# Key-value products of a gated linear recurrence: row tiles of 64 tokens with 112 columns in place of four quarter tiles

## The chip, the cores and the metric

The kernel runs on one core of a Trainium2 chip. The metric is the device time of one execution in microseconds, the median of several runs. A core has a matrix engine (TensorE, in the profile PE, with its weight loads as PEld), a vector engine (VectorE, DVE), a scalar engine (ScalarE, ACT), a general engine (GpSimd, POOL) and a queue engine (SyncE, SP) which here issues most DMAs. Each engine works through its own instructions in order and waits on the others by semaphores.

## The reference

Two blocks follow each other: a gated recurrence with complex gates, for 4 batches, 8 heads, 768 tokens and 48 numbers a head, and a mixer with a low-rank product over the tokens and a two-layer product over the channels. Cut to its core:

```python
for t in range(S):                     # gates a normalised to a magnitude of at most 0.999
    new_re = ar * S_re - ai * S_im
    new_im = ar * S_im + ai * S_re
    kv = np.einsum('bhd,bhe->bhde', k[:, :, t], v[:, :, t])
    S_re, S_im = (new_re + kv, new_im)
    y[:, :, t] = np.einsum('bhd,bhde->bhe', q[:, :, t], S_re)
x = y.transpose(0, 2, 1, 3).reshape(B, S, H * D)
...
h = x.transpose(0, 2, 1) @ U @ V                      # U: 768 x 32, V: 32 x 768
u = x + h.transpose(0, 2, 1)
out = u + np.maximum(u @ w_ch1, 0.0) @ w_ch2          # 384 -> 1536 -> 384
```

## The kernel before

The recurrence is done in chunks of 128 tokens: 6 chunks for each of 4 batches, 24 in all, each for all 8 heads. Gates become running phases and magnitudes; queries and keys are multiplied by them, so that what is left in a chunk are plain products. For a chunk the steps are:

- `prep`: VectorE weighs q and k and makes QKC, which has for every token and head two parts u = 0, 1 (48 numbers each, one for the cosine, one for the sine), each in a place of 64 columns, so that the two parts stand in columns 0 to 47 and 64 to 111; columns 48 to 63 hold zeros. TensorE turns it (`tr`, line 816) in row tiles of 64 tokens: two tiles, one for each half of the chunk, side by side in the array.
- `inner` (line 845): products of keys and queries within each half, masked by VectorE into AT.
- `state` (line 865): the key-value products, the step that is changed. For each head h and half r, the weights are k's 64 tokens by a part's columns and the moving operand is the values' 64 tokens by 48 numbers (VP). The sum over the 64 tokens goes to dk[r], rows 0 to 63 for part 0 and rows 64 to 111 for part 1. It is issued in two operations of 4 heads each. In the last chunk of a batch only half 0 is needed. The array is used as four tiles of 64x64, (half, part).
- VectorE adds dk[0] and dk[1] to the running state G, with the state at the middle of the chunk in GM (for the first chunk of a batch, ScalarE copies GM instead).
- `y` (lines 894 and 902): products of AT with the values and of the queries with the states, copied by ScalarE into xo.

The mixer takes two chunks at a time (groups m = 0 to 11): `rank` and `mixed` (lines 937 and 960) for the low-rank part, `rT` and `rw` for a correction of the first group, `uTp` for the turned input, then the two-layer product. Group 0 does it plainly; from group 2 on, `few` (line 1103) does the first layer with fewer products, and from group 1 on `down_two` (line 1235) does the second layer with fewer products out of sums of the weights; VectorE makes these sums, one of them at line 1305 for the first such group (m = 1), in place over a part of w2.

The order of the work is written out by hand, or rather by a planner before: every step is added to a list with its engine, an estimated cost, and `way`, the form in which it splits TensorE's array (0 the whole array, 1 column tiles, 3 four quarter tiles, 4 row tiles of 32, 5 row tiles of 64). `ORDER` is the order in which the 2210 listed operations are emitted, on all engines; the estimates stand in the code but play no part in the emitted program. `SPARE` names operations before which dummy products on an identity matrix are emitted (`idle`, lines 1383 and 1387); 34 of them in all.

A tile takes part in the semaphores by the framework's own account of reads and writes; the lists of reads and writes in the plan only check the order.

Of the kernel before, what the change touches and what calls it, by code (L numbers as in the profile page):

```python
# [19 lines left out]
HC = CH // 2  # L20
# [94 lines left out]
)  # L115

SPARE = {
    125: 2, 135: 10, 199: 14, 209: 1, 223: 5, 243: 2,
}

DUMP = None
# [195 lines left out]
def kernel(  # L317
# [15 lines left out]
    nc = tc.nc  # L333
    B, H, S, D = q.shape
    DP = 64
# [1119 lines left out]
```

## Time and profile before

| | us |
|---|---|
| median of 3 runs | 555.26 (554.55 to 555.47) |
| the profiled execution | 554.71 |
| its span, first to last instruction | 552.8 |
| TensorE busy in the span | 526.9 (95%) |
| VectorE busy | 432.8 (78%) |
| ScalarE busy | 317.8 (57%) |
| GpSimd busy | 32.2 (6%) |
| mean granted TensorE clock | 0.998 |

How the profile's views are read: in the page's 40 slices a digit is the busy share of a slice in tenths. Groups of instructions have the line, engine, operation, output and inputs by name, the shape (for a product the weights' rows*columns, then the moving operand's rows and columns), the count, and then the busy time in us, the mean duration of one in ns, and the idle time before them with what ended it. The chain of work that ended last, in order of time, has a start in us, a length in us, and what it was. A row of waits names who waited for whom, the us in total, the number of times and the longest. A timeline has a start, a length, and the instructions merged in it. Products are pipelined: one of 0.22 us may start 0.015 us after another.

### The profile page before, as it was taken

What the parts mean: (1) busy time and instruction counts of PE and PEld (TensorE: products, weight loads), DVE (VectorE), ACT (ScalarE), POOL (GpSimd) and SP (SyncE); (2) the same over time, 40 slices, a digit from 0 to 9 for tenths busy, and PEclk for the clock granted to TensorE, in tenths of its full rate; (3) what the DMA queues carried; (4) which work ended last, traced back from release to release, by engine and by line L of the source; (5) the groups of instructions that cost most, each with busy time, mean ns of one, the idle gap of its engine ahead of it and who ended that gap; (6) DMA issues with size and microseconds to landing.
All of it is one profiled execution on the core that took longest, in us unless ns stands there. A gap on an engine that the chain in (4) does not pass through costs nothing.

```text
span 552.8 us, 16672 instructions
## 1 busy us (share of the span) xinstructions
PE 526.9 (95%) x7228; PEld 477.3 (86%) x7228; DVE 432.8 (78%) x828; ACT 317.8 (57%) x553; POOL 32.2 (6%) x61
## 2 busy tenths in 40 slices
PE   2899999999999999999999999999999999999996
PEld 1677776767999987999999998999999989999995
DVE  6899989999999987998787987786953635567352
ACT  6889999795597787567827956626512232110100
POOL 1000000001010000102001001002000000000000
PEclk9999999999999999999999999999999999999999
DMA  9988876523441354314513425003300000000001
GB/s 229 187 184 174 195 170 151 144 30 87 88 89 30 56 104 77 59 31 85 91 38 67 74 38 111 2 1 59 59 9 23 17 11 15 8 8 23 21 9 34
DMA packets 150688, 39.92 MB, mean 72 GB/s; under 512 B 145912, under 2 KB 147408, under 8 KB 150608
## 3 DMA queue, kind: packets, MB, share of 16 engines
q1 hardware_dynamic: 148400, 34.43, 31.2%
q0 software_dynamic: 2208, 4.35, 2.3%
q8 instruction: 59, 0.97, 0.7%
q14 instruction: 21, 0.17, 0.1%
HBM read 33.60 MB, written 4.76 MB: 69 GB/s over the span
## 4 chain that ended last, share of the span: by engine, by line
PE 73%; DVE 12%; ACT 4%; issue 2%; DMA 1%; POOL 0%; DVEq 0%; SPq 0%; ACTq 0%; POOLq 0%
PE down L1235 26%; PE few L1103 25%; PE tr L816 4%; PE dk L865 3%; PE inner L845 3%; PE y L902 3%; PE up L991 2%; PE y L894 2%; DVE xo L444 1%; ACT gate L438 1%; PE rank L937 1%; PE ph L755 1%; PE mixed L960 1%; PE uTp L976 1%; PE es ps L691 1%
## 5 line engine op out<-in xcount | busy, mean ns | idle before, releaser
L1111 ACT COPY h<-few 128x512 f32<-128x512 f32 x60 | 35.1, 585 | 87.3 <-PE few L1103 87.1
L1235 PE MATMUL down<-w,h 128*128 128x192 f32 x396 | 72.7, 330 | 0.9 <-DVE xo L444 0.7
L438 ACT ACTIVATE gate<-gate 128x768 f32<-128x768 f32 (+2 forms) x74 | 65.6, 900 | 9.2 <-DVE GS L750 3.8
L1235 PEld LDWEIGHTS down<-w,h 128*128 128x128 f32 x396 | 64.5, 190 | 3.7 <-issue 1.5
L822 ACT COPY QK<-tr 112x512 f32<-112x512 f32 x96 | 49.9, 596 | 17.8 <-PE tr L816 17.7
L444 DVE TENSOR_TENSOR xo<-down,xo 128x192 f32<-128x192 f32 (+1 forms) x79 | 29.9, 385 | 33.9 <-PE down L1235 33.4
L1115 DVE CUSTOM_DVE_ANT_1 h<-few,h 128x512 f32<-128x512 f32 x60 | 40.5, 686 | 15.7 <-PE few L1103 11.8
L1103 PE MATMUL few<-extra,w 128*128 128x128 f32 x400 | 50.9, 276 | 0.0
L1103 PEld LDWEIGHTS few<-extra,w 128*128 128x128 f32 x400 | 48.0, 192 | 0.1
L441 DVE TENSOR_TENSOR QKC<-qk,cs 128x768 f32<-128x768 f32 x48 | 44.4, 950 | 1.7 <-PE dk L865 1.3
L1235 PE MATMUL down<-stage 128*128 128x192 f32 x198 | 37.9, 330 | 0.4 <-DVE xo L444 0.4
L438 ACT ACTIVATE es<-es ps 128x384 f32<-128x384 f32 x48 | 20.1, 502 | 31.2 <-PE es ps L691 29.2
L444 DVE TENSOR_TENSOR h<-few,h 128x512 f32<-128x512 f32 x30 | 20.6, 688 | 20.4 <-ACT h L1111 12.1
L1179 POOL DMA_DIRECT2D out_dram<-xo x32 | 17.9, 558 | 313.8 <-DVE xo L444 297.7
L991 PE MATMUL up<-uT,w 128*128 128x256 f32 x144 | 34.5, 387 | 0.7 <-ACT uT L980 0.7
L1235 PEld LDWEIGHTS down<-stage 128*128 128x128 f32 x198 | 32.3, 190 | 1.7 <-DVE xo L444 1.0
L1103 PE MATMUL few<-gate,w 128*128 128x128 f32 x240 | 32.2, 278 | 0.4 <-DVE gate L1075 0.4
L435 ACT ACT_TABLE_LOAD x24 | 30.8, 1283 | 1.1 <-PEq L1439 0.7
L816 PEld LDWEIGHTS tr<-ident,QKC 64*112 64x112 f32 x768 | 24.2, 130 | 8.3 <-issue 3.6
L816 PE MATMUL tr<-ident,QKC 64*112 64x64 f32 x768 | 28.9, 221 | 2.4 <-DVE QKC L441 2.4
L991 PEld LDWEIGHTS up<-uT,w 128*128 128x128 f32 x144 | 26.4, 190 | 5.3 <-ACT uT L980 0.9
L1103 PEld LDWEIGHTS few<-gate,w 128*128 128x128 f32 x240 | 29.3, 192 | 0.8 <-PE uTp L976 0.6
(161 smaller groups left out, 1100.4 us busy)
## 6 DMA issues: line engine op xcount, KB each, us to landing
stage<-in_moe_w_ch_dram SPq DMA_DIRECT2D x12, 768.0 KB
gate<-in_a_im_dram SPq DMA_DIRECT2D x24, 192.0 KB
gate<-in_a_re_dram SPq DMA_DIRECT2D x24, 192.0 KB
VP<-in_v_dram SPq DMA_DIRECT2D x24, 192.0 KB
qk<-in_q_dram SPq DMA_DIRECT2D x24, 192.0 KB
qk<-in_k_dram SPq DMA_DIRECT2D x24, 192.0 KB
out_dram<-xo POOLq DMA_DIRECT2D x12, 192.0 KB, 2.2
out_dram<-xo POOLq DMA_DIRECT2D x20, 96.0 KB, 2.1
```

What stands on the lines that cost most here:

```text
L435: ACT(1.4, rank, lambda: nc.scalar.preload_act_table_set(name), writes=[TABLE])
L438: return nc.scalar.activation(out=o, in_=i, func=f, **kw)
L441: nc.vector.tensor_tensor(out=o, in0=a, in1=b, op=OP.mult)
L444: nc.vector.tensor_tensor(out=o, in0=a, in1=b, op=OP.add)
L816: nc.tensor.transpose(out=get(*ps[r])[0:DQ, h], in_=get(*qkc)[at, h].rearrange("p u d -> p (u d)")[:, 0:DQ], identity=ident[at, at], tile_ ...
L822: nc.scalar.copy(out=get(*QK)[:, u].rearrange("p (h t) -> p h t", t=CH)[:, :, r * HC:(r + 1) * HC], in_=get(*ps[r])[0:DQ])
L991: nc.tensor.matmul(out=get(*ps)[:, e], lhsT=w1[:, f, (ff + e) * 128:(ff + e + 1) * 128], rhs=get(*uT)[:, f], start=(f == 0), stop=(f == KD ...
L1103: nc.tensor.matmul(out=get(*ps)[:, q], lhsT=w()[:, q * 128:(q + 1) * 128], rhs=v[0](), start=(n == 0 and q == 0), stop=True, skip_group_ch ...
L1111: ACT(c_act(n3 * CH) - 0.045, RU, lambda i=i, k=k: nc.scalar.copy(out=at(i, k), in_=get(*ps)), [ps], [o])
L1115: DVE(c_dve(n3 * CH), RU, lambda i=i, k=k: nc.vector._custom_dve(dve_ops.TENSOR_ADD_SAT, out=at(i, k), in0=get(*ps), in1=at(i, k), s0=math ...
L1179: queue.dma_start(out=out[b, c * CH:(c + 1) * CH, lo:hi], in_=get("xo", i)[:, lo:hi])
L1235: nc.tensor.matmul(out=get(*to)[:, part], lhsT=x(j), rhs=y[:, j], start=(first and j == 0), stop=(j == KH - 1), skip_group_check=not first)
```

## The change

The state products are no longer four tiles for each head but two: the two parts of a head, with the 16 columns of zeros between them, are taken as one operand of 112 weight columns, and the two halves of the chunk stand as row tiles of 64 tokens side by side, as in the transposes of line 816. The outputs are the same rows of dk[r]; rows 48 to 63 now hold zeros from the product itself.

```diff
             for h in range(h0, h0 + HH):
                 for r in parts_k:
                     at = slice(r * HC, (r + 1) * HC)
-                    for x, end in ((0, DP), (DP, DQ)):
-                        nc.tensor.matmul(out=get(*dk[r])[x:end, h], lhsT=get(*ks)[at, h, x // DP, 0:end - x], rhs=get(*VPi)[at, h],
-                                         start=True, stop=True, tile_position=(r * HC, x))
+                    nc.tensor.matmul(out=get(*dk[r])[0:DQ, h], lhsT=get(*ks)[at, h].rearrange("p u d -> p (u d)")[:, 0:DQ],
+                                     rhs=get(*VPi)[at, h], start=True, stop=True, tile_position=(r * HC, 0))
         for h0 in (0, HH):
-            PE(0.443, RR, lambda h0=h0: state(h0), [ks, VPi], [dk[r] + (h0,) for r in parts_k], way=3,
-               steps=4 * HH * len(parts_k),
+            PE(0.4, RR, lambda h0=h0: state(h0), [ks, VPi], [dk[r] + (h0,) for r in parts_k], way=5,
+               steps=2 * HH * len(parts_k),
                takes=[mid_G] + ([] if last else [G]))
```

The order of all work is replaced by another one made for these estimates, of the same 2210 operations. On TensorE 505 of 624 operations stand at another place of its list, by 7 places in the mean and 56 at most; on VectorE 667 of 793, on ScalarE 422 of 553, on GpSimd 15 of 48, on SyncE 143 of 192. The dummy products are 32 instead of 34:

```diff
 SPARE = {
-    125: 2, 135: 10, 199: 14, 209: 1, 223: 5, 243: 2,
+    125: 3, 135: 10, 199: 15, 209: 1, 227: 2, 253: 1,
 }
```

One product of `down_two` names a further read, so that it comes after the vector operation of line 1305, which makes the weights it uses:

```diff
             onto(ub, 1, two, 0)
-            product(one, 0, lambda j: of(0, 1)[:, j], w2_of(0, 1), names, first=False)
+            product(one, 0, lambda j: of(0, 1)[:, j], w2_of(0, 1), lambda half: names(half) + [("w2", 0)], first=False)
             onto(ub, None, one, 0)
```

169 rows, old and new, of the table ORDER are left out of this document.

## The prediction

> **What bounds the kernel now.** I read first the page's busy shares and its 40 slices, then the chain that ended last, then what TensorE waited for.
>
> ```profile
> span 552.8 us, 16672 instructions
> PE 526.9 (95%) x7228; PEld 477.3 (86%) x7228; DVE 432.8 (78%) x828; ACT 317.8 (57%) x553; POOL 32.2 (6%) x61
> PE   2899999999999999999999999999999999999996
> DVE  6899989999999987998787987786953635567352
> ACT  6889999795597787567827956626512232110100
> PEclk9999999999999999999999999999999999999999
> PE 73%; DVE 12%; ACT 4%; issue 2%; DMA 1%; POOL 0%; DVEq 0%; SPq 0%; ACTq 0%; POOLq 0%
> ...
> PE es ps L695 <- DVE GL L444: 11.0, 1, 11.0
> PE tr L816 <- DVE QKC L441: 2.4, 3, 1.6
> PE ph L758 <- ACT gate L438: 1.4, 3, 0.8
> PE down L1235 <- DVE xo L444: 1.3, 4, 0.7
> PE ph L761 <- DVE F L764: 1.2, 2, 0.6
> PE dk L865 <- issue: 0.8, 2, 0.5
> PE up L991 <- ACT uT L980: 0.7, 1, 0.7
> PE ph L755 <- PE tr L816: 0.4, 1, 0.4
> ...
> PE down L1235 <- issue: 0.2, 1, 0.2
> ```
>
> TensorE is busy in 95% of the span, nine tenths in each slice but the first and last few, at a granted clock that never falls, and 73% of the chain is its own. Of what it waited for, 11.0 us is the wait for the first gates before its first product. All others of that list come to about 10 us (2.4 + 1.4 + 1.3 + 1.2 + 0.8 + 0.7 and, from the row of 0.4 to that of 0.2, six small ones of 2.0 in all). So from 11 us on TensorE is a queue that is hardly ever empty. A change of its own work goes nearly whole into the time, and the question is only what the key-value products cost in each form.
>
> **What they cost now.** Each of the 8 heads of a chunk has two halves of 64 tokens (r) and two parts (x, with 64 and 48 columns of weights). The rows by shape say in how many instructions each product is issued:
>
> ```profile
> L865 PE MATMUL dk<-VP,QKC 64*64 64x48 f32 x704 | 27.7, 221 | 0.3 <-issue 0.3
> L865 PE MATMUL dk<-VP,QKC 64*48 64x48 f32 x704 | 24.9, 214 | 0.5 <-issue 0.5
> ...
> 160.97 1.07 PE dk L865 x56
> 236.90 2.00 PE dk L865 x120
> 446.15 1.99 PE dk L865 x89
> ```
>
> 20 chunks do both halves and the last chunk of each of 4 batches one: 8 x (20 x 2 + 4) = 352 products of each part, and 704 instructions, so two passes for each. A chunk is thus 64 instructions (the chain keeps some 56 of them), and takes 1.07 us when it stands alone; two chunks in a row take 2.00. So the work itself is 0.93 us, 0.058 for each group of four instructions that run side by side on the four 64x64 tiles, and 0.14 us is the entry and exit of a run. The last row is a whole chunk and a last one: 1.99 - 1.07 = 0.92 for a last chunk, although it has half the instructions. A group with two tiles idle thus takes as long as one with four; what counts is groups. Sum now: 20 x 0.93 + 4 x 0.92 = 22.3 us.
>
> **What they cost after.** One product now has 112 weight columns, 64 rows, and the same 48 moving columns. Two of them (r = 0 and 1) stand side by side. A chunk is 8 heads x 2 passes = 16 groups, as before; the number of instructions halves (1408 to 704), that of groups stays at 24 x 16 = 384. So everything hangs on the time of a group. No row has a plain product of this form; these are nearest:
>
> ```profile
> L816 PEld LDWEIGHTS tr<-ident,QKC 64*112 64x112 f32 x768 | 24.2, 130 | 8.3 <-issue 3.6 <-DVE QKC L441 2.5 <-DVE xo L444 0.2
> L976 PEld LDWEIGHTS uTp<-ident,xo 128*128 128x128 f32 x72 | 8.5, 141 | 2.8 <-DVE xo L444 0.8 <-ACT QK L822 0.6 <-ACT es L438 0.4
> L865 PEld LDWEIGHTS dk<-VP,QKC 64*48 64x48 f32 x704 | 21.8, 119 | 0.0
> L865 PEld LDWEIGHTS dk<-VP,QKC 64*64 64x64 f32 x704 | 24.6, 135 | 3.0 <-issue 1.4 <-DVE AT L848 0.2
> L960 PEld LDWEIGHTS mixed<-r,V 64*128 64x128 f32 x96 | 8.1, 186 | 1.9 <-ACT r L943 0.8 <-issue 0.6 <-PE ph L755 0.3
> L1005 PEld LDWEIGHTS rT<-both,r 64*128 64x128 f32 x6 | 0.8, 188 | 0.0
> L1005 PE MATMUL rT<-both,r 64*128 64x32 f32 x6 | 0.7, 258 | 0.0
> ...
> 92.28 0.41 PEld L1005 LDWEIGHTS rT<-both,r 64*128 64x128 f32 x3
> 96.46 0.30 PEld L960 LDWEIGHTS mixed<-r,V 64*128 64x128 f32 x4 [0.17 <-issue]
> ...
> 49.18 1.04 PE tr L816 x32
> 309.64 1.48 PE tr L816 x48
> 251.99 0.89 PE few L1103 x8
> ```
>
> Weight loads of plain products grow with their columns: 119 ns for 48, 135 for 64, 186 to 188 for 128, about 0.8 ns a column, and the number of rows makes no difference (rT and mixed have 64 rows). How often a tile can take one is the next row: three loads of rT, 128 columns each, last 0.41 us; less the 0.188 of the last one that is two steps of 0.111, though their products move only 32 columns (64x32 in the row of rT's products). The "few" products have 128 weight columns and 128 moving ones and take 0.89 / 8 = 0.111 as well. So with few moving columns the load sets the step: 0.111 at 128 columns, 0.058 at 64. In a straight line between these, 112 columns give 0.058 + 48/64 x 0.053 = 0.098 us. The two halves do load side by side: four loads of mixed, two for each half, are over in 0.30 us, which is one step of 0.111 and a last load of 0.186; one after another they would need 0.52.
>
> The transposes of line 816 have the very shape, 64x112, and cost (1.48 - 1.04) / 8 = 0.055 for a pair. But they are no measure: their load of 112 columns takes 130 ns, less than the 135 of a plain one of 64, and the transposes of line 976 load 128 columns in 141 where plain products need 186 and more. A transpose loads at about half price. I take 0.098 and keep 0.055 (the transposes) and 0.111 (all of 128 columns) as ends.
>
> Sum after: 384 x 0.098 = 37.6 us, 15.3 more than now. With the ends: 384 x 0.055 = 21.1 (1.2 less) and 384 x 0.111 = 42.6 (20.3 more).
>
> **The other parts of the change.** The order of all work is new. I counted neighbours in the list of TensorE's 624 operations whose form of tiling (the number "way" in the code) differs: 160 before and 147 after, where a state operation counts as row tiles like the transposes. A run of dk has 0.14 us for its two ends, 0.07 for each: 13 x 0.07 = 0.9 us gained. Against it, a run of plain row tiles is dearer to enter:
>
> ```profile
> 213.31 0.88 PE mixed L960 x8
> 475.95 1.50 PE mixed L960 x16
> ```
>
> 8 instructions more are 0.62 us here, so 0.26 lie at the ends, 0.12 more than for dk. 29 of the 48 ends of dk runs still meet another form, 29 x 0.06 = 1.7 us; since mixed has 128 columns and a longer stream I take 1.0 (0 to 1.7). The dummy products between operations (SPARE) go from 34 to 32, each of two instructions of 0.111: 0.4 us gained.
>
> The added dependence on ("w2", 0) makes one product of the second mixer group wait in the plan for the vector subtraction at line 1305; that one keeps its place in the list (594th before, 593rd after), the product too (701st, 704th), 100 operations later. It costs nothing. Should that distance go, the product would stand behind one vector operation of 1.27 us:
>
> ```profile
> 132.48 1.27 DVE w L1305
> ```
>
> What waits for the state products is the vector engine's sum GM; it ends at most 0.64 us later for each chunk (16 x 0.098 - 0.93), and that sum's readers are later TensorE work in the same queue, which is late by as much. So nothing else becomes late by it. The other engines do gain: VectorE at 78% and ScalarE at 57% have 15 us more for the same work, so some waits of TensorE shrink. All those waits after the first product are 10 us; many follow TensorE's own products (xo from down) and stay. I take 2 us for this and for what the new order does to waits, between 0 and 10; a new order can lose as well, and its planner put a state operation at 0.4 us where I expect 0.78 (8 x 0.098), so I give it no gain beyond.
>
> The sum, against the profiled execution's own 554.7 us (552.8 of span and 1.9 around it; the median of the runs is 555.3, 0.5 higher and inside their spread): 554.7 + 15.3 - 0.9 + 1.0 - 0.4 - 2.0 = 567.7. I predict 567.5 us, 2.2% slower.
>
> **The rivals.** *The load is as cheap as the transposes'.* Then a group takes 0.055, and the time is 554.7 - 1.2 - 0.9 - 0.4 = 552.2 (551 to 554.5): faster. It decides at one place, the step of two row tiles with 112 weight columns: below (22.3 + 1.3) / 384 = 0.061 us the kernel is faster, above it slower. For it speaks the same shape in line 816; against it the loads of rT and mixed, plain products in the same row tiling, at 186 to 188 ns. [...]
>
> *The loads don't overlap.* If the second half's load or the second pass's waits for the first's, a group takes up to 0.196; for whole chunks 20 x 16 x 0.196, for last ones 4 x 16 x 0.098, together 69.0 us, and the time is 554.7 + 46.7 - 1 = about 600. Against it: the four loads in 0.30 us. A form of it with part of the load in sight would end between 575 and 600.
>
> *The work is hidden.* If the waits shrink by all of their 10 us, or the new order saves as much, the time is 567.7 - 8 = about 559.5 (557 to 560.5, since other terms can be a little less). Against it: the slices of TensorE are full to the end, while VectorE's and ScalarE's are at 7 tenths and less in the last ten, so that there is little left there for it to wait for.
>
> **Chances.** Forecast, a step set by a load of 112 columns and mostly in sight: 0.82, with 560 to 573. As cheap as the transposes or as before: 0.10. Loads in a row, wholly or in part: 0.04. Hidden: 0.04. The range 559.5 to 573 holds the first and some of the last: its low end has 8 us of waits gone, its high end the dear step of 0.111 (20.3 instead of 15.3). A difference below 0.2%, 1.1 us, can't be told from no change here. Faster by more is the cheap load, 0.08; within it 0.02, where that case is eaten by the order; slower 0.90.
>
> **What would show it.** Profile after: dk in one group, 704 weight loads of 64x112 of about 175 ns (135 + 48 x 0.83), against 130 if the cheap load holds. The chain's runs of one chunk at about 1.6 to 1.8 us, two in a row some 1.57 more (cheap: 0.9; in a row: 3.1). TensorE still at 95% or more, with its waits at 10 us less a few. The prediction is wrong if that step is below 0.09 or above 0.115 us, or if the waits change by over 5 us either way.

## The result, and the profile after

| | us |
|---|---|
| before, median of 4 runs beside the changed kernel | 555.37 (554.55 to 557.82) |
| changed, median of 4 runs | 567.76 (566.60 to 571.68) |
| ratio | 1.0229, 95% interval 1.0201 to 1.0256 |
| changed, another time, 4 runs against 13 of before | 568.28 against 555.95, ratio 1.0247 (1.0210 to 1.0283) |
| profiled executions of the changed kernel | 571.68 (span 569.9) and 566.08 (span 564.3) |

The change costs 12.4 us. First the page of the first profiled execution: the span, TensorE's busy time, its 40 slices and its granted clock, and the two rows of the state products, now in one form.

```profile
span 569.9 us, 15239 instructions
PE 544.6 (96%) x6520; PEld 495.6 (87%) x6520; DVE 434.9 (76%) x828; ACT 319.0 (56%) x553; POOL 32.1 (6%) x61
PE   2799998999999999999999999999999999999996
PEclk9978999999999999999999999999999999999999
L865 PE MATMUL dk<-VP,QKC 64*112 64x48 f32 x704 | 43.6, 265 | 0.4 <-ACT gate L439 0.4
L865 PEld LDWEIGHTS dk<-VP,QKC 64*112 64x112 f32 x704 | 41.0, 180 | 2.9 <-ACT gate L439 1.0
```

Half as many products and loads (704 instead of 1408), and 43.6 us of busy time where the two old forms had 27.7 and 24.9, which overlapped. TensorE is as full as it was, so that it still bounds the kernel. New is the granted clock: it falls in the third and fourth slice. In the second profiled execution it falls only once before the end, and that is the cleaner one to read the steps from. Its weight loads, its chain in order of time (start, us, what) and its waits:

```profile
L865 PEld LDWEIGHTS dk<-VP,QKC 64*112 64x112 f32 x704 | 39.6, 174 | 2.9 <-ACT gate L439 1.0 <-issue 1.0
...
247.24 3.28 PE dk L865 x64
282.69 1.56 PE dk L865 x32
287.96 1.70 PE dk L865 x32
...
PE es ps L696 <- DVE GL L445: 10.1, 1, 10.1
PE tr L817 <- DVE QKC L442: 2.8, 2, 2.5
PE ph L759 <- ACT gate L439: 1.2, 1, 1.2
```

A chunk that stood alone with 1.07 us now takes 1.70, or 1.56 where it follows the transposes, whose tiling it shares. Two in a row take 3.28: 1.58 for a chunk, 0.098 to 0.099 for each of its 16 groups. A weight load takes 174 ns, where the 135 ns of 64 columns and 48 more columns at 0.83 ns had given 175; the transposes' load of the same shape had 130 before. The wait for the first gates is 10.1 us, 0.9 less than before.

### The profile page after: what moved, and what is told of

Read it like the earlier page. It is cut to its first block, busy times and chain, and to the rows that moved or that the text cites. A ratio compares the mean times of both kernels' runs of the same rounds, so it can differ in the third digit from the quotient of the medians.

```text
span 569.9 us, 15239 instructions
## 1 busy us (share of the span) xinstructions
PE 544.6 (96%) x6520; PEld 495.6 (87%) x6520; DVE 434.9 (76%) x828; ACT 319.0 (56%) x553; POOL 32.1 (6%) x61
## 4 chain that ended last, share of the span: by engine, by line
PE 70%; issue 11%; ACT 4%; DVE 4%; DMA 2%; POOL 1%; POOLq 0%; DVEq 0%; ACTq 0%
PE down L1235 22%; PE few L1103 19%; PE dk L865 5%; PE up L991 5%; PE inner L846 3%; PE down L1192 3%; PE tr L817 3%; PE y L902 2%; DMA gate<-F 2%; ACT gate L439 2%; PE y L894 2%; PE mixed L960 1%; PE uTp L976 1%; PE ph L759 1%; PE ph L756 1%
## 5 line engine op out<-in xcount | busy, mean ns | idle before, releaser
L823 ACT COPY QK<-tr 112x512 f32<-112x512 f32 x96 | 50.2, 596 | 28.2 <-PE tr L817 27.9
L865 PE MATMUL dk<-VP,QKC 64*112 64x48 f32 x704 | 43.6, 265 | 0.4 <-ACT gate L439 0.4
L865 PEld LDWEIGHTS dk<-VP,QKC 64*112 64x112 f32 x704 | 41.0, 180 | 2.9 <-ACT gate L439 1.0
L817 PEld LDWEIGHTS tr<-ident,QKC 64*112 64x112 f32 x768 | 26.5, 138 | 6.9 <-DVE QKC L442 3.4
```

The source lines that it names most:

```text
L817: nc.tensor.transpose(out=get(*ps[r])[0:DQ, h], in_=get(*qkc)[at, h].rearrange("p u d -> p (u d)")[:, 0:DQ], identity=ident[at, at], tile_ ...
L823: nc.scalar.copy(out=get(*QK)[:, u].rearrange("p (h t) -> p h t", t=CH)[:, :, r * HC:(r + 1) * HC], in_=get(*ps[r])[0:DQ])
L865: nc.tensor.matmul(out=get(*dk[r])[0:DQ, h], lhsT=get(*ks)[at, h].rearrange("p u d -> p (u d)")[:, 0:DQ], rhs=get(*VPi)[at, h], start=True ...
```

## The experiments

Seven runs were made, the changed kernel once more and six other kernels; each has its ratio to the kernel before on the same chip.

**The changed kernel again.** No edit.

> The changed kernel once more, for a second profile and as the base of the runs beside it. Theory L (the load of 112 weight columns sets a step of 0.098 us, and nearly all of 384 x 0.040 = 15.3 us is in sight): 566 to 569 us, TensorE's step for a pair of row tiles 0.098. The first profile showed a granted clock of 0.73 between 25 and 50 us; theory C (the change itself lowers the clock at the start, by more waits there): low again, clock at most 0.99 in every profile; theory L has no need of it: clock above 0.995 in some.

568.28 us, ratio 1.0247. The step is 0.098 (above). The granted clock of the eight executions of the changed kernel so far was 0.987 to 0.997, never above, against 0.995 to 1.000 in all but one of the 13 of before taken with them (that one had 0.946 and 563.33 us). So 566 to 569 held, and the 0.995 was reached in some, against theory C; yet there is a loss of clock that theory L doesn't know. The stretches around the one fall of the second profile (length, then busy time and count by engine, then the granted clock, the share of the DMA engines and GB/s):

```profile
25.00:28.70 3.70, 2.65 (x52) 2.50 (x54) 3.70 (x6) 3.12 (x5) 0.00 (x0) 1.00 1.36 233
28.75:32.10 3.35, 3.35 (x48) 3.00 (x46) 2.77 (x7) 2.93 (x5) 0.00 (x0) 0.50 1.05 277
32.20:40.00 7.80, 6.84 (x158) 5.60 (x154) 7.36 (x15) 5.89 (x11) 0.00 (x0) 1.00 0.89 192
```

The clock is halved for one stretch of 3.4 us, right after the first chunk's state products, and then whole again. They need not be the cause: in the first profile the fall begins at 25.7 us, ahead of the first state product at 27.8.

**The form in the old order.** The changed state products, with ORDER and SPARE as before. The operation's estimate and the further read of `down_two` are those of the changed kernel too; the cut shows the products alone. Against the kernel before:

```diff
                     at = slice(r * HC, (r + 1) * HC)
-                    for x, end in ((0, DP), (DP, DQ)):
-                        nc.tensor.matmul(out=get(*dk[r])[x:end, h], lhsT=get(*ks)[at, h, x // DP, 0:end - x], rhs=get(*VPi)[at, h],
-                                         start=True, stop=True, tile_position=(r * HC, x))
+                    nc.tensor.matmul(out=get(*dk[r])[0:DQ, h], lhsT=get(*ks)[at, h].rearrange("p u d -> p (u d)")[:, 0:DQ],
+                                     rhs=get(*VPi)[at, h], start=True, stop=True, tile_position=(r * HC, 0))
```

> The new form of the key-value products in the order and with the dummy products of before. Theory L: the whole loss is the form's: +15.3 for the load, -1.2 for 17 changes of tiling form fewer (143 against 160, 0.07 us each), +1.0 for dearer entries, -2 of waits: 567 to 569 us. Rival O (part of the loss is the new order's, which was made for a cost of 0.4 us where it is 0.78): at least 3 us below the changed kernel. Rival P (the new order pays part of the form back): at least 3 us above it.

567.52 us, ratio 1.0218 (1.0144 to 1.0292): the changed kernel's time, 0.8 us below its median. Its four executions lie in two pairs, 565.26 and 565.34 at a clock of 1.000 and 569.71 and 571.74 at 0.990 and 0.987, so that the interval is wide, 8 to 16 us. The median has neither O nor P, which asked for 3 us below or above: most of the loss is the form's, but this run alone can't tell a share of 3 us. Its executions also have 2.7 to 3.1 us outside the span, where those of the other kernels have 1.8 or 1.9; why isn't known. By the mean spans the form alone costs 11.3 us (565.1 against 553.8).

**The new order with the old form.** The reverse: the new ORDER and SPARE with the four quarter tiles. Against the changed kernel:

```diff
                     at = slice(r * HC, (r + 1) * HC)
-                    nc.tensor.matmul(out=get(*dk[r])[0:DQ, h], lhsT=get(*ks)[at, h].rearrange("p u d -> p (u d)")[:, 0:DQ],
-                                     rhs=get(*VPi)[at, h], start=True, stop=True, tile_position=(r * HC, 0))
+                    for x, end in ((0, DP), (DP, DQ)):
+                        nc.tensor.matmul(out=get(*dk[r])[x:end, h], lhsT=get(*ks)[at, h, x // DP, 0:end - x], rhs=get(*VPi)[at, h],
+                                         start=True, stop=True, tile_position=(r * HC, x))
```

> The four quarter tiles of before in the new order, with the new dummy products. Theory L: as before, 555 us within 1.5 (165 changes of tiling form against 160 cost 0.35, two dummy products fewer save 0.4). Rival O: 558 and more. Rival P: 552.5 and less.

557.17 us over 10 runs against 555.95, ratio 1.0031 (1.0010 to 1.0053). The order alone costs 1.2 us by the medians and 0.6 to 2.9 by the interval: small, but not nothing, and the median is inside the 1.5 that L allowed and less than O gave. The two parts, 2.2% and 0.3%, are together what the change shows, within the intervals; by the mean spans they are 11.3 and 1.6 us, and the changed kernel's is 12.7. The stretch from 25 to 50 us in this kernel's profile (length, busy time and count by engine, clock, DMA):

```profile
25.00:50.00 25.00, 21.62 (x411) 17.05 (x412) 23.63 (x40) 20.79 (x38) 0.00 (x0) 0.93 0.98 205
```

The clock falls here with the quarter tiles too (3.4 us at a half, from 26.5 us on). So a fall in the first 50 us needs no new form.

**16 more weight columns.** The changed kernel, all 128 columns of a place as weights:

```diff
-                    nc.tensor.matmul(out=get(*dk[r])[0:DQ, h], lhsT=get(*ks)[at, h].rearrange("p u d -> p (u d)")[:, 0:DQ],
+                    nc.tensor.matmul(out=get(*dk[r])[0:128, h], lhsT=get(*ks)[at, h].rearrange("p u d -> p (u d)"),
```

> The changed kernel, its state products with all 128 columns of the place as weights (16 more, which are zeros, and 16 more rows of zeros in the result, not used). Theory L: the step goes from 0.098 to 0.111 us, 384 x 0.013 = 5.0 us more than the changed kernel, 571 to 573 us; weight loads of 187 ns. Rival S (the step belongs to two row tiles as such, whatever the columns): no more than the changed kernel, within 1 us.

576.68 us, ratio 1.0376 (1.0342 to 1.0411). The loads by form, the chain and the clock of its profile:

```profile
L865 PEld LDWEIGHTS dk<-VP,QKC 64*128 64x128 f32 x704 | 47.1, 196 | 2.9 <-issue 1.1 <-ACT gate L439 1.0
...
252.22 4.06 PE dk L865 x64
295.21 1.92 PE dk L865 x32
...
PEclk9989999999999999989999998999999999999999
...
252.00:255.30 3.30, 3.30 (x64) 3.23 (x62) 3.30 (x5) 0.84 (x1) 0.00 (x0) 1.00 0.59 113
255.45:258.80 3.35, 3.35 (x18) 3.26 (x17) 1.67 (x3) 2.50 (x4) 0.00 (x0) 0.50 0.02 3
```

A chunk is 1.92 instead of 1.70: 0.22 / 16 is 0.014 more a step, and 0.098 + 0.014 = 0.112. Outside the stretches of half clock a load takes 187.5 ns, against the 187 expected; the 196 of the row has the others in it. S has fallen. The time is 8.4 us above the changed kernel's, not 5.0; 384 x 0.014 = 5.4 is the step's. The rest goes with the clock: 0.981 to 0.988 in its executions, and the rows show where. Two chunks that stand in a row took 4.06 us; TensorE was busy all the while (3.30 of 3.30 us from 252.00), and from 255.4 us, 3.2 us into them, the clock was halved for 3.4 us. The chunks' own last steps ran at that clock, and so did the products after them.

**16 more moving columns.** The changed kernel, and the one with 128 weight columns, with 64 moving columns (of the edit, only the moving operand is shown):

```diff
-                                     rhs=get(*VPi)[at, h], start=True, stop=True, tile_position=(r * HC, 0))
+                                     rhs=get(*VPi)[at].rearrange("p h d -> p (h d)")[:, h * D:h * D + n], start=True, stop=True,
+                                     tile_position=(r * HC, 0))
```

Here n is 64, or 48 for the last head, and dk keeps its whole place of 64 columns a head, of which the sums read 48.

> The changed kernel, its state products with 64 moving columns where they had 48 (16 of the next head's values more; their results aren't used; the last head keeps 48). Theory L (the load of 112 weight columns sets the step, the moving columns run behind it): the step stays 0.098, the time 566 to 569 us or less. Rival M (load and moving columns add up in part): 16 columns at 0.83 ns are 13 ns, 384 x 0.013 = 5 us more, 571 to 573. Theory H (the clock is halved for 3.4 us at a time after long runs of state products, since the array multiplies in only 0.040 of each 0.098 us): it multiplies in 0.053 now, so no halving after the first 50 us and clocks of 0.995 and more.

568.11 us, ratio 1.0241 (1.0207 to 1.0274). The chain of this kernel:

```profile
248.55 3.28 PE dk L866 x64
284.02 1.57 PE dk L866 x32
289.29 1.70 PE dk L866 x32
```

The same three rows as with 48 columns, to 0.01 us. M has fallen: the moving columns run behind the loads. H isn't borne out: no fall of the clock after 50 us stands in this profile, but none stands in the changed kernel's two either, and its four executions had 0.988 to 0.996, like the changed kernel's.

> 128 weight columns and 64 moving ones in the state products (the added results aren't used). Theory L: a step of 0.111 as with 128 weight columns alone, 5 us above the changed kernel, 571 to 573 us. Theory H: with 128 weight columns alone the profile showed four halvings of 3.4 us and two of twice that; here the array multiplies in 0.053 of 0.111 us instead of 0.040, so fewer of them, a clock of 0.993 and more and 3 us less than that kernel's 576.7. Rival M: as much as that kernel or more, 576 to 581.

One of its four executions took 3089.61 us, of which no profile was taken and whose cause isn't known; the other three had 572.93, 576.33 and 577.81. Ratio 1.0359 (1.0317 to 1.0401). Its step is that of 128 weight columns (a chunk alone 1.92 us again), which is L's. Two of the three times lie in M's 576 to 581, but the step, which M would have made longer, has not grown. The profile with 48 moving columns has, before its end, two falls of 3.4 us and two of twice that, not four and two as was expected here; this one has two of 3.4 and one of twice that. The clock was 0.985 to 0.993, a little above the 0.981 to 0.988 with 48 moving columns, but the time isn't the 571 to 573 of L nor clearly the 3 us less of H.

**Loads of 32 columns.** The kernel before, its products cut into eight tiles of 64 tokens by 32 columns:

```diff
-                    for x, end in ((0, DP), (DP, DQ)):
-                        nc.tensor.matmul(out=get(*dk[r])[x:end, h], lhsT=get(*ks)[at, h, x // DP, 0:end - x], rhs=get(*VPi)[at, h],
-                                         start=True, stop=True, tile_position=(r * HC, x))
+                    for x in range(0, DQ, 32):
+                        n = min(32, DQ - x)
+                        nc.tensor.matmul(out=get(*dk[r])[x:x + n, h], lhsT=get(*ks)[at, h].rearrange("p u d -> p (u d)")[:, x:x + n],
+                                         rhs=get(*VPi)[at, h], start=True, stop=True, tile_position=(r * HC, x))
```

> The kernel before, in its own order, with the state products cut the other way: eight tiles of 64 tokens by 32 weight columns (32, 32, 32 and 16) instead of four. Theory L: a load of 32 columns is 0.83 x 32 = 27 ns and a few, so it sets nothing any more; the 48 moving columns do, 0.040 and some: a step of 0.043 to 0.046, 384 x 0.012 to 0.015 = 4.6 to 5.8 us less than before, 549.5 to 551 us. Rival I (instructions of one group follow each other by 6 to 7 ns, as the pairs of the transposes' and the queries' rows do): 8 x 7 = 0.056, no gain, 554 to 556. Rival S (a group costs 0.058 whatever it holds): no gain.

598.08 us, ratio 1.0751 (1.0726 to 1.0776), which none of the three had. Its page's clock, its rows by form and two stretches of TensorE's timeline:

```profile
PEclk9989999999899989989999999999999988999999
...
L866 PE MATMUL dk<-VP,QKC 64*32 64x48 f32 x2112 | 34.2, 215 | 15.5 <-issue 15.5
L866 PEld LDWEIGHTS dk<-VP,QKC 64*32 64x32 f32 x2112 | 29.4, 108 | 18.7 <-issue 17.2
...
173.49 1.36 PE L866 MATMUL dk<-VP,QKC 64*32 64x48 f32 x128
...
260.02 1.48 PE L866 MATMUL dk<-VP,QKC 64*32 64x48 f32 x130
263.19 1.47 PE L866 MATMUL dk<-VP,QKC 64*32 64x48 f32 x126 [1.70 <-issue]
```

A load now takes 108 ns (105 outside the stretches of half clock), about 0.9 ns a column less than one of 64 columns. But a whole chunk, 128 products, lasts 1.36 us; less the 0.21 of the last one that is 0.072 for a group of eight, where the four tiles had 0.058. By the starts of the single products, the second and third group of nearly every such run take 0.042 and 0.043, which is what L gave for 48 moving columns, the next two some 0.10 and 0.13, and most of the others 0.066 to 0.068: one product, with its load, in 8.4 ns. That is rival I's kind of limit, dearer than its 0.056. (In the trace of before, neighbours in the queries' rows start 6 to 7 ns apart, those in the transposes' mostly 3 to 4.) On top of it TensorE stood still in or before state products, 13 times and 20.9 us in all (15.5 of it before those of 32 columns), and waited for nothing that the profile shows, as for 1.70 us in the last row. A chunk has 256 instructions here, loads included, 128 in the old form and 64 in the new. That the instructions come too slowly fits this, but it wasn't tested by itself. The clock also fell in six places between 30 and 500 us. So the load, which allowed a step of 0.042 us in the second and third groups, isn't the bound here any more, and the kernel is slower for other reasons, the stops of 20.9 us foremost.

## Why the prediction was right

It gave 567.5 us (559.5 to 573); measured was 567.76.

*The step of a group.* This was the term everything hung on, and it came out as said: 0.098 us (0.098 to 0.099 measured), out of a load of 174 ns (175 said). Three experiments bear it: 16 weight columns more make a step of 0.112, 16 moving columns more change it by nothing, and the form alone in the old order has most of the loss. That moving columns set the step where they take longer shows in other products of the kernel before: those of `down`, with 128 weight columns and 192 moving ones, follow each other by 0.163 us, those of `up`, with 128 and 256, by 0.216, where the 128 and 128 of `few` took 0.111. The work is 24 x 16 x 0.098 = 37.6 us against 22.3, as predicted. The cheap load of the transposes, the main rival, would have shown 130 ns, and loads one after another a chunk of 3.1; neither is there. The 0.055 of the transposes, which the prediction kept as an end, is no price of their load: they move 64 columns, and the products of `inner`, with 64 weight and 64 moving columns, step by 0.058 too. Two statements of the prediction have their measure in rows that it doesn't print. Plain loads of 128 columns take 190 ns with 128 rows (`down`), 186 with 64 (`mixed`) and 184 with 32 (line 1031), so that the rows hardly count. And loads of a single column take 80 to 82 ns (lines 1374 and 1375): from there the transposes' 112 columns add some 50 ns to reach 130, where the plain ones of the changed kernel add some 94 to reach 174: a transpose's "about half price".

*The ends of a run.* Here the sum was wrong by 2 us. It gained 0.9 for 13 changes of tiling form and lost 1.0 for dearer entries. To see what was gained, I added in the trace the times from each TensorE product to the next one, by the name of the first. The state products with the wait behind them have 28.2 us before and 39.3 in the second profile of the changed kernel:

| | before | changed | difference |
|---|---|---|---|
| the groups themselves | 22.3 | 37.7 | +15.4 |
| two dummy products | 0.4 | 0.4 | 0 |
| ends of runs and waits behind them | 5.5 | 1.2 | -4.3 |
| sum | 28.2 | 39.3 | +11.1 |

Of the 5.5 us, 22 runs x 0.14 = 3.1 are ends, and 2.4 are three runs that waited, at 61.7, 137.5 and 198.7 us. The entry isn't dearer: a chunk alone has 1.70 - 1.57 = 0.13 at its ends, as the 0.14 before; the row of mixed, from which the 1.0 was taken, was no measure for it. And the gain of fewer changes of form wasn't the new order's, as the prediction had it. In the old order with the new form I count 143 changes, fewer than the 147 of the changed kernel, and the new order with the old form has 165. It is the form that makes neighbours of the transposes and the state products, and 19 of their 48 borders need no change now.

*The waits.* 2.0 us were taken off, out of the 10 us of waits after the first product. The waits of TensorE that the profile names are 20.8 us in all before and 18.8 in the second profile. That is 2.0 less, but 0.9 of it is the wait for the first gates, and those after it shrink only from 9.8 to 8.7. The 2.4 us at the state products are gone, and others stand in their place, such as 0.8 us before `y`, which the new order with the old form has too.

*The clock.* That it falls wasn't in the sum at all. Between the fastest of the changed kernel's eight executions (566.08) and their median (568.28) lie 2.2 us, and they go with the clock: 566.1 to 566.7 us at 0.996 and 0.997, 570.5 to 571.7 at 0.987 and 0.988.

The spans of the two profiled executions, 552.8 and 564.3 us, are 11.5 apart: 15.4 for the groups, -1.9 for the ends, -2.4 for the waits at the state products, and +0.4 for all else that TensorE does, added up in the same way. What the new order costs is within that 0.4 and isn't added again. The medians are 12.4 apart, 1.0 more than these two executions (566.08 - 554.71 = 11.4): the changed kernel's median is 1.7 above its profiled execution, with lower clocks in the slower ones, that of the kernel before 0.7.

The prediction had 15.3 for the groups, +0.1 for the ends, -0.4 for the dummy products and -2.0 for the waits, 13.0 in all. Its main term is right by its mechanism and its size. That the median came within 0.3 us of the centre is luck: the ends were put 2.0 us too dear, and the 1.7 us of the slower executions, which the sum left out, made up for most of that.

## What to carry to other kernels

Small products side by side in the array were paid for by the group here, and a group took the longer of its widest weight load (for plain float products 0.058 us at 64 columns and 0.098 at 112, some 0.83 ns a column) and its moving columns (0.163 us for the 192 of `down`), as long as no other limit came in, as it did with eight tiles. Merging two tiles into a wider one halved the instructions (1408 to 704) and lengthened the load (135 to 174 ns). By this it lost here: with 48 or 64 moving columns the step was 0.098 us all the same. Where the moving side takes longer than the new load, merging should lose nothing by the load; that is an estimate from these steps, and the case wasn't run. A transposing product was no measure for a plain one of the same shape: its load took 130 ns against 174, and its step was 0.055 us against 0.098.

## What the hardware showed that was not expected

The granted clock was halved in spells of 3.4 us, or two or three times that. The first profile of the changed kernel has two of them ahead of its end, one of 10.2 us from 25.7 us on and one of 3.4 us from 42.8 us on; the clock is 0.50 in both, and 1.00 between them and after them up to the end. What sets their length was not shown.

The spells of the first 50 us need no new form: every profile but that of the kernel before has one there, and TensorE was busy in only 0 to 2.7 of the 3.4 us ahead of them (1.2 and 2.7 us in the first profile of the changed kernel). The later ones are another matter. The profiles with 112 or 128 weight columns have six of them: one with 112 in the old order, three with 128, two with 128 and 64 moving columns. The profiles with quarter tiles have none, nor have the other three with 112. State products stand ahead of all six, and ahead of five TensorE counted as busy in the whole 3.4 us (3.30 of 3.30 us in the row at 252.00). So busy time as the profile counts it didn't keep the clock up there. By an estimate the array multiplies in 0.040 us of each step of 0.098 or 0.112 (48 columns at 0.83 ns, from the 0.216 us of `up`'s 256 moving columns and the 0.163 of `down`'s 192); that this is what counts was not shown, since 64 moving columns didn't clearly help. Nor is it the length of the load alone. Over the executions the clock was 0.994 to 1.000 with quarter tiles in the new order, 0.987 to 1.000 with 112 columns and 0.981 to 0.988 with 128, but 0.968 to 0.976 with eight tiles, whose loads are the shortest (108 ns); there TensorE had stood still for half of the time ahead of each spell after 50 us (busy 1.4 to 1.8 of 3.4 us).

The second thing is how small products with eight tiles are limited: 0.042 us a group for the second and third of a run, then 0.067 for most, and stops of 0.5 to 3.6 us within the runs. So this tiling, fast in its first steps, lost all of it there: 598.08 us, ratio 1.0751.
